# A spectral filter and a gated unit: four-channel words in the relayout, tables by TensorE, set-up inside the plan

## The chip, the cores and the metric

The kernel runs on one core of one Trainium2 chip. The metric is device microseconds of one execution, as the median of several. A core has TensorE (PE, with its weight loads as PEld), VectorE (DVE), ScalarE (ACT), GpSimd (POOL) and SyncE (SP). Here SP issues stores and on-chip relays by DMA, and POOL issues the loads that change type.

## What is computed

The reference filters along the sequence in the frequency domain, then applies a gated linear unit with a causal convolution of five taps in its gate.

```python
X = np.fft.rfft(x, axis=1)                       # x: 8 x 3200 x 256
F = (filt_r + 1j * filt_i)[None, :, :]           # 1601 x 256
x = np.fft.irfft(X * F, n=3200, axis=1)
xp = np.concatenate([zeros(8, K - 1, 256), x], axis=1)   # K = 5
gate = 1 / (1 + exp(-sum_k conv_w[k] * xp[:, k:k + S, :]))
out = (gate * (x @ w_val)) @ w_out
```

## The kernel before, in words

Each of the 8 batches is 3200 x 256. The sequence index is split as 100 x 32 (L = 100, R = 32), and the transform is done in two stages on either side of the filter, all with matmuls against tables of sines.

Stage A of a batch:

- x comes in eight chunks (j) of four of the 32 residues, cast to bf16 (`load_x`, L160, issued by POOL; ten buffers).
- s1 (L369) multiplies a chunk by the table cf_t: two matmuls of 512 columns. Their moving operand is x seen as words of two neighbouring channels: for each channel pair, four residues, two channels, so it is read in contiguous runs of two bf16 values. The result is evicted by `so` (ACT L360 or DVE L362) into the tile so, laid out as channel pair, residue, channel.
- Four transposes of DVE (`turn`, L387) take a pair of bf16 channels as one fp32 word and exchange 32 residues with 32 partitions, from so into tt.
- s2 (L397) multiplies by w_t, per unit of two frequencies (seven units, u = 0 to 6, the last of one): eight matmuls of 256 columns on quarters of the array. They too read runs of two values. `xs` evicts; `zed` (L415) multiplies by the two filter tiles fr_t and fi_t into za and zb; `inva` (L428) multiplies by a_t and b_t; `ue` evicts; `wr` (L449, SP) writes to a scratch in DRAM, escr.

Stage B of a batch, eight chunks again:

- `lv` (L459, L460, SP) loads vt from escr, six buffers; ib (L469) multiplies by ci_t; `ye` (L479, ACT) evicts into y; `halo` copies the edge on POOL.
- `conv` (L496) is the gate's convolution by diagonal matrices dg_t; `gate` (L505, ACT) the sigmoid; `val` (L514) the product with w_val; `gv` (L524, DVE) their product; `outp` (L534) the product with w_out; `oe` evicts and `store` (L548, L549, SP) writes the output.

The order of the work of every engine is fixed when the program is built. A planner (`Plan`) simulates the tasks with costs written by hand, ranks (batches and chunks staggered), pools of buffers and times for data to land, and gives one order; each engine then executes its own part of it in that order. PSUM has four buffers of 1024 fp32, shared by all products.

Ahead of the planned part stands `setup`, emitted as a whole: the iotas and all DMA issues on POOL; on DVE the index arithmetic for cf_t, w_t, a_t, b_t and ci_t; sines on ACT. The tables w_t, a_t and b_t are each 128 x 1664: a sum of index terms (on DVE for w_t; for a_t and b_t on POOL, from a product gg that POOL makes, L272, and additions, L250, tiles tba and tbb), rounded off by three DVE steps (L208 twice, L214), and a sine. cf_t has its zeros set by four memsets of POOL (L225 to L228), which stand behind the filter loads in POOL's order. The filters come in by eight loads of POOL (L198, L200; 16 rows of 26 frequencies, every second row of the filter, forward and reversed) and four copies by SP (L203). The diagonals are 20 small multiplies of DVE (L345). The planner knows of all this only as one task, `setup`, with a landing time of 22 us, and POOL as free at 18 us.

Of the kernel before, what the change touches and what calls it, by code (L numbers as in the profile page):

```python
# [16 lines left out]
L = 100  # L17
# [85 lines left out]
def kernel(  # L103
# [25 lines left out]
    DP = D // 2  # L129
# [5 lines left out]
    a_t = cpool.tile([128, NS, 64], FP16, name="a_t")  # L135
    b_t = cpool.tile([128, NS, 64], FP16, name="b_t")
# [26 lines left out]
    gstack = ExitStack()  # L163
    g1 = gstack.enter_context(tc.tile_pool(name="gen", bufs=1, side="right"))
# [7 lines left out]
    def col(name):  # L172
        return g1.tile([128, 1], FP32, name=name)

    def setup():
        pcol = iota([128, 1], [[0, 1]], 0, "pcol", 1)
        k1f = iota([128, 2, 2, 32], [[26, 2], [0, 2], [1, 32]], 0, "k1f")
        phf = iota([128, 2, 2, 32], [[0, 2], [25, 2], [0, 32]], 25, "phf")
        for j in range(4):
            load_x(0, j)  # L180
        ki = iota([128, NS], [[1, NS]], 0, "ki")
        k2w = g1.tile([128, 2, 32], FP32, name="k2w")
        iota(None, [[0, 2], [1, 16]], 0, None, dst=k2w[:, :, 0:16])
        iota(None, [[0, 2], [-1, 16]], 31, None, dst=k2w[:, :, 16:32])
        cw2 = iota([128, 2, 32], [[1, 2], [0, 32]], 0, "cw2")
        rr = iota([128, 2, 32], [[0, 2], [1, 32]], 0, "rr")
        for j in range(4, NCH):
            load_x(0, j)
        af = iota([128, L], [[1, L]], 0, "af")
        hm = iota([128, NS], [[2, NS]], 0, "hm")  # L190

        def fsrc(f, row, ap):
            return bass.AP(tensor=f.tensor, offset=f.offset + row * D, ap=ap + [[1, D]])

        for f, dst in ((filt_r, fr_t), (filt_i, fi_t)):
            fv = dst[...].rearrange("p h m d -> p (h m) d")
            for t in range(2):
                nc.gpsimd.dma_start(out=fv[64 * t:64 * t + 16],  # L198
                                    in_=fsrc(f, t, [[100 * D, 16], [2 * D, NS]]))
                nc.gpsimd.dma_start(out=fv[64 * t + 16:64 * t + 32],  # L200
                                    in_=fsrc(f, 100 - t, [[100 * D, 16], [-2 * D, NS]]))
            for t in range(2):
                nc.sync.dma_start(out=fv[64 * t + 32:64 * t + 64], in_=fv[64 * t:64 * t + 32])  # L203

        V = nc.vector

        def ts(o, i, s, op):
            V.tensor_scalar(o, i, s, None, op0=op)  # L208

        def frac(t, n, shape):  # L210
            y = g1.tile(shape, FP32, name=f"fy{n}")
            ts(y[...], t[...], MAGIC, ALU.add)
            ts(y[...], y[...], MAGIC, ALU.subtract)
            V.tensor_tensor(y[...], t[...], y[...], op=ALU.subtract)  # L214
            return y

        idx = g1.tile([128, 2, 2, 32], FP32, name="idx")
        V.scalar_tensor_tensor(idx[...], k1f[...], pcol[:, 0:1], phf[...], op0=ALU.mult,
                               op1=ALU.add)
        ts(idx[...], idx[...], 0.01, ALU.mult)  # L220
        f = frac(idx, "f", [128, 2, 2, 32])
        nc.scalar.activation(cf_t[...].rearrange("p h c i -> p (h c i)"),
                             f[...].rearrange("p h c i -> p (h c i)"), AF.Sin,
                             scale=6.2831850)
        nc.gpsimd.memset(cf_t[:, :, :, NS:32], 0.0)  # L225
        nc.gpsimd.memset(cf_t[:, 0, 1, 0:1], 0.0)
        nc.gpsimd.memset(cf_t[:, 1, 1, 24:25], 0.0)
        nc.gpsimd.memset(cf_t[:, 1, :, 25:26], 0.0)  # L228

        ge = []  # L230
        for i, v in enumerate((31.5, 63.5, 95.5)):
            t = col(f"ge{i}")
            ts(t[...], pcol[...], v, ALU.is_ge)
            ge.append(t)
        hi = ge[1]
        cc, lo, q16 = col("cc"), col("lo"), col("q16")
        V.tensor_tensor(cc[...], ge[0][...], ge[1][...], op=ALU.subtract)
        V.tensor_tensor(cc[...], cc[...], ge[2][...], op=ALU.add)
        ts(lo[...], cc[...], -32.0, ALU.mult)
        V.tensor_tensor(lo[...], lo[...], pcol[...], op=ALU.add)  # L240
        V.scalar_tensor_tensor(lo[...], hi[...], -64.0, lo[...], op0=ALU.mult, op1=ALU.add)
        ts(q16[...], lo[...], 15.5, ALU.is_ge)
        k2p = col("k2p")
        V.tensor_scalar(k2p[...], lo[...], -2.0, 47.0, op0=ALU.mult, op1=ALU.add)
        V.tensor_tensor(k2p[...], k2p[...], q16[...], op=ALU.mult)
        V.tensor_tensor(k2p[...], k2p[...], lo[...], op=ALU.add)

        def table(dst, e1, e2, name, adder):
            t = g1.tile([128, NS, 64], FP32, name="tb" + name)
            adder.tensor_tensor(t[...], e1, e2.unsqueeze(1).to_broadcast((128, NS, 64)),  # L250
                                op=ALU.add)
            y = frac(t, "t", [128, NS, 64])
            nc.scalar.activation(dst[...].rearrange("p s k -> p (s k)"),
                                 y[...].rearrange("p s k -> p (s k)"), AF.Sin,
                                 scale=6.2831850)

        e1 = g1.tile([128, NS], FP32, name="e1")
        h26 = col("h26")
        ts(h26[...], hi[...], 26.0, ALU.mult)
        V.tensor_scalar(e1[...], ki[...], h26[:, 0:1], lo[:, 0:1], op0=ALU.add, op1=ALU.mult)  # L260
        ts(e1[...], e1[...], 1.0 / N, ALU.mult)
        e2 = g1.tile([128, 2, 32], FP32, name="e2")
        wph = col("wph")
        V.tensor_scalar(wph[...], cc[...], -0.25, 0.25, op0=ALU.mult, op1=ALU.add)
        V.tensor_scalar(e2[...], k2w[...], lo[:, 0:1], 1.0 / R, op0=ALU.mult, op1=ALU.mult)
        V.scalar_tensor_tensor(e2[...], cw2[...], 0.25, e2[...], op0=ALU.mult, op1=ALU.add)
        ts(e2[...], e2[...], wph[:, 0:1], ALU.add)
        table(w_t, e1[...].unsqueeze(2).to_broadcast((128, NS, 64)),
              e2[...].rearrange("p c k -> p (c k)"), "w", V)

        gg = g1.tile([128, NS, 64], FP32, name="gg")
        nc.gpsimd.tensor_tensor(  # L272
            gg[...], hm[...].unsqueeze(2).to_broadcast((128, NS, 64)),
            rr[...].rearrange("p c k -> p (c k)").unsqueeze(1).to_broadcast((128, NS, 64)),
            op=ALU.mult)
        ts(gg[...], gg[...], 1.0 / N, ALU.mult)
        kp, aph = col("kp"), col("aph")
        V.scalar_tensor_tensor(kp[...], k2p[...], 100.0, hi[...], op0=ALU.mult, op1=ALU.add)
        ts(kp[...], kp[...], 1.0 / N, ALU.mult)
        V.tensor_scalar(aph[...], cc[...], 0.25, 0.25, op0=ALU.mult, op1=ALU.add)  # L280
        ea = g1.tile([128, 2, 32], FP32, name="ea")
        eb = g1.tile([128, 2, 32], FP32, name="eb")
        V.tensor_scalar(ea[...], rr[...], kp[:, 0:1], aph[:, 0:1], op0=ALU.mult, op1=ALU.add)
        V.scalar_tensor_tensor(ea[...], cw2[...], -0.25, ea[...], op0=ALU.mult, op1=ALU.add)
        bph = col("bph")
        V.tensor_scalar(bph[...], q16[...], 0.5, 0.25, op0=ALU.mult, op1=ALU.add)
        ts(eb[...], ea[...], bph[:, 0:1], ALU.add)
        table(a_t, gg[...], ea[...].rearrange("p c k -> p (c k)"), "a", nc.gpsimd)
        table(b_t, gg[...], eb[...].rearrange("p c k -> p (c k)"), "b", nc.gpsimd)

        vg = iota([128, 1], [[0, 1]], 0, "vg", 1)
        vi, vh, vc = col("vi"), col("vh"), col("vc")
        ii = g1.tile([128, 1], I32, name="ii")
        ts(ii[...], vg[...], 1.0, ALU.mult)
        ij = g1.tile([128, 1], I32, name="ij")

        def bits(o, shift, mask):
            src = ii
            if shift:
                ts(ij[...], ii[...], shift, ALU.logical_shift_right)  # L300
                src = ij
            if mask:
                ts(ij[...], src[...], mask, ALU.bitwise_and)
            V.tensor_copy(o[...], ij[...])
        bits(vi, 2, 0)
        bits(vh, 1, 1)
        bits(vc, 0, 1)
        kv, ph, wt, mt = col("kv"), col("ph"), col("wt"), col("mt")
        V.scalar_tensor_tensor(kv[...], vh[...], 26.0, vi[...], op0=ALU.mult, op1=ALU.add)
        V.tensor_scalar(ph[...], vc[...], 25.0, 25.0, op0=ALU.mult, op1=ALU.add)  # L310
        V.tensor_scalar(wt[...], kv[...], 50.5, 2.0, op0=ALU.is_lt, op1=ALU.mult)
# [356 lines left out]
```

## Time and profile before

| what | us |
|---|---|
| runs | 378.3, 375.16, 382.08 |
| median | 378.3 |
| profiled execution, own time | 377.58 |
| its span | 375.8 |
| PE busy | 308.6 |
| DVE busy | 279.3 |
| ACT busy | 267.5 |
| POOL busy | 71.3 |
| mean granted clock of TensorE | 0.928 |

The span runs from the first to the last instruction of the profiled execution; its own time has a little around it. In a row of the timeline the first number is the start from the span's beginning and the second the time that the group took; instructions overlap in their engine's pipeline, so the distance between two starts is what one costs in a row of them. [...] The granted clock is a share of full speed.

### The profile page before, as it was taken

Reading aid. Unit: us, or ns where it says so; the run is one execution under the profiler, and the core shown is the slowest. Engines: PE = TensorE matmul, PEld = TensorE weight load, DVE = VectorE, ACT = ScalarE, POOL = GpSimd, SP = SyncE. Lnnn points to the kernel's source line nnn. Section 1 sums busy time; section 2 is a strip of 40 time slices with the busy share of each in tenths; the row PEclk is TensorE's granted clock in tenths of the full one; section 3 lists DMA queues with packets and bytes.
Section 4 is the critical chain, followed back from the end, with each engine's and each line's share of the span. In section 5 each row is a group of like instructions: output and inputs, shape, how many; then the busy total and the mean of one; then the engine's idle time right before and its main releaser. Section 6 shows DMA issues by size and latency. Waiting matters only on the chain.

```text
span 375.8 us, 9658 instructions
## 1 busy us (share of the span) xinstructions
PE 308.6 (82%) x3936; PEld 190.5 (51%) x3936; DVE 279.3 (74%) x365; ACT 267.5 (71%) x302; POOL 71.3 (19%) x128
## 2 busy tenths in 40 slices
PE   0340158496999999899999999899999999999993
PEld 0000013124656675466656665567566767777662
DVE  8299987889457898487878797779697989834531
ACT  1231138586879797678878997789788978887673
POOL 9696612030112110210021101200010001001000
PEclk9985558877899999899999999999999999999998
DMA  7999979479679986989779986985485548868644
GB/s 111 148 127 154 153 134 165 137 113 261 186 186 233 258 212 154 221 245 211 195 145 260 246 220 144 262 250 164 143 255 153 165 144 269 238 178 242 202 129 136
DMA packets 57997, 70.91 MB, mean 189 GB/s; under 512 B 8160, under 2 KB 38368, under 8 KB 57824
## 3 DMA queue, kind: packets, MB, share of 16 engines
q1 hardware_dynamic: 44896, 55.20, 49.7%
q0 software_dynamic: 13056, 15.08, 31.2%
q8 instruction: 31, 0.51, 0.6%
q14 instruction: 14, 0.11, 0.1%
HBM read 43.78 MB, written 39.85 MB: 223 GB/s over the span
## 4 chain that ended last, share of the span: by engine, by line
PE 55%; DVE 21%; DMA 9%; ACT 5%; issue 4%; POOL 3%; SPq 1%; POOLq 0%; ACTq 0%; DVEq 0%
PE ps L534 13%; PE ps L496 11%; PE ps L369 9%; PE ps L514 7%; DMA vt<-escr 7%; DVE tt L387 7%; PE ps L397 6%; PE ps L469 5%; PE ps L428 4%; DVE gv L524 4%; DVE dg_t L345 3%; DMA xt<-in_x_dram 2%; ACT so L360 2%; DVE so L362 1%; ACT o L360 1%
## 5 line engine op out<-in xcount | busy, mean ns | idle before, releaser
L369 PE MATMUL ps<-xt,cf_t 100*128 100x512 bf16 x128 | 64.5, 609 | 36.2 <-DVE so L362 18.7
L524 DVE TENSOR_TENSOR gv<-ps,gt 128x800 bf16<-128x800 f32 x64 | 62.7, 981 | 23.1 <-PE ps L514 14.8
L360 ACT ACTIVATE so<-ps 128x1024 bf16<-128x1024 f32 x50 | 51.1, 1024 | 40.1 <-PE ps L369 25.8
L362 DVE CAST xs<-ps 128x1024 bf16<-128x1024 f32 (+1 forms) x44 | 50.5, 1147 | 35.2 <-PE ps L397 34.7
L360 ACT ACTIVATE o<-ps 100x1024 f32<-100x1024 f32 x59 | 60.7, 1028 | 18.5 <-PE ps L534 14.2
L534 PE MATMUL ps<-wo_t,gv 128*100 128x256 bf16 x512 | 69.0, 278 | 1.5 <-DVE gv L524 1.0
L160 POOL DMA_DIRECT2D xt<-in_x_dram x64 | 36.9, 579 | 158.1 <-PE ps L369 156.2
L496 PE MATMUL ps<-yt,dg_t 64*64 64x400 bf16 x1280 | 66.6, 337 | 0.0
L534 PEld LDWEIGHTS <-gv 128*100 128x100 bf16 x512 | 54.3, 126 | 21.6 <-issue 12.7
L505 ACT ACTIVATE gt<-ps 128x800 bf16<-128x800 f32 x64 | 53.6, 839 | 4.6 <-PE ps L496 3.7
L479 ACT ACTIVATE yt<-ps 128x800 bf16<-128x800 f32 x64 | 53.2, 837 | 4.7 <-PE ps L469 4.6
L514 PE MATMUL ps<-yt,wv_t 128*128 128x400 bf16 x256 | 53.9, 333 | 0.0
L360 ACT ACTIVATE u<-ps 128x1024 bf16<-128x1024 f32 (+1 forms) x46 | 44.6, 975 | 6.0 <-PE ps L428 3.2
L469 PEld LDWEIGHTS <-vt 104*128 104x128 bf16 x512 | 31.1, 102 | 30.9 <-issue 22.2
L397 PE MATMUL ps<-tt,w_t 64*64 64x256 bf16 x416 | 36.0, 412 | 12.9 <-DVE tt L387 10.1
L496 PEld LDWEIGHTS <-dg_t 64*64 64x64 bf16 x1280 | 33.7, 107 | 16.4 <-issue 2.8
L387 DVE STREAM_TRANSPOSE tt<-so 128x1024 f32<-128x1024 f32 x32 | 38.7, 1227 | 2.7 <-ACT so L360 2.6
L369 PEld LDWEIGHTS <-cf_t 100*128 100x128 f16 x128 | 12.0, 104 | 56.0 <-DMA xt<-in_x_dram 19.6
L469 PE MATMUL ps<-ci_t,vt 104*128 104x100 f16 x512 | 34.5, 213 | 5.5 <-DMA vt<-escr 5.5
L415 DVE TENSOR_TENSOR za<-xs,fr_t 128x1024 bf16<-128x1024 bf16 (+1 forms) x56 | 36.1, 649 | 3.5 <-ACT xs L360 2.3
L415 DVE TENSOR_TENSOR zb<-xs,fi_t 128x1024 bf16<-128x1024 bf16 (+1 forms) x56 | 35.5, 640 | 0.0
L428 PE MATMUL ps<-zb,b_t 64*64 64x256 bf16 x416 | 28.2, 279 | 4.4 <-DVE zb L415 4.4
(106 smaller groups left out, 222.4 us busy)
## 6 DMA issues: line engine op xcount, KB each, us to landing
out_dram<-o SPq DMA_DIRECT2D x64, 384.0 KB
xt<-in_x_dram POOLq DMA_DIRECT2D x64, 200.0 KB, 6.1
escr<-u SPq DMA_DIRECT2D x48, 256.0 KB
vt<-escr SPq DMA_DIRECT2D x64, 192.0 KB
escr<-u SPq DMA_DIRECT2D x8, 128.0 KB
vt<-escr SPq DMA_DIRECT2D x64, 16.0 KB
out_dram<-o SPq DMA_DIRECT2D x64, 16.0 KB
fr_t<-in_filt_r_dram POOLq DMA_DIRECT2D x4, 208.0 KB, 11.5
```

The source lines that it names most:

```text
L360: nc.scalar.activation(dst, src, AF.Copy, **kw)
L362: nc.vector.tensor_copy(dst, src)
L369: nc.tensor.matmul(ps[:, 512 * h:512 * h + 512], lhsT=cf_t[0:L].rearrange("p h c i -> p (h c i)"), rhs=xv[:, 64 * h:64 * h + 64], start=Tr ...
L387: nc.vector.transpose(dst, src)
L397: nc.tensor.matmul(ps[64 * t:64 * t + 64, 512 * h + D * a:512 * h + D * a + D], lhsT=w_t[rows, i, :], rhs=t_[rows, :, i, :], start=True, s ...
L415: (nc.vector if e == "DVE" else nc.gpsimd).tensor_tensor(z[:, :, 0:nm * D], xs_[:, :, 0:nm * D], f[:, :, m0:m0 + nm, :].rearrange("p h m d ...
L469: nc.tensor.matmul(ps[:, o:o + L], lhsT=v[0:NV, a, 128 * dh:128 * dh + 128], rhs=ci_t[0:NV, :], start=True, stop=True)
L496: nc.tensor.matmul(ps[64 * dh:64 * dh + 64, 512 * r:512 * r + RC * L], lhsT=dg_t[rows, dh, k, :], rhs=y[rows, dh, RC * j + k:RC * j + k + ...
L505: nc.scalar.activation(g[...], ps[:, :].rearrange("p (h n) -> p h n", h=2)[:, :, 0:RC * L], AF.Sigmoid)
L514: nc.tensor.matmul(ps[:, 512 * eh:512 * eh + RC * L], lhsT=wv_t[:, dh, 128 * eh:128 * eh + 128], rhs=y[:, dh, H + RC * j:H + RC * j + RC, ...
L524: nc.vector.tensor_tensor(gv_[...], ps[:, :].rearrange("p (h n) -> p h n", h=2)[:, :, 0:RC * L], g[...], op=ALU.mult)
L534: nc.tensor.matmul(ps[0:L, D * a:D * a + D], lhsT=gv_[:, eh, L * a:L * a + L], rhs=wo_t[:, eh, :], start=(eh == 0), stop=(eh == 1))
```

## The change

Six things change together.

1. Words of four channels (E = 4) instead of two in s1's moving operand, in the layouts of so and tt, and so in s2's moving operand, which are now read in runs of four values. The transposes still take fp32 words; source and destination are seen as channel quad, word of the quad, residue, so the innermost step is two words.
2. Of the three tables only w_t is made from index terms. Frequencies are numbered by half (t) and then in order, in place of alternately. a_t and b_t come from w_t by matmuls with a small matrix j2 (identity and a signed swap), and are evicted in four pieces each, b_t with a sign per row.
3. The 20 multiplies for dg_t become two with broadcast operands. Rounding is one fused step in place of two. cf_t's zeros are set on its argument, by DVE.
4. The filters are loaded in two cuts (6 and 7 of 13 frequencies per half), by 32 loads on POOL in place of 8, half of them contiguous; eight copies by SP in place of four.
5. The set-up's steps are tasks of the planner with ranks, costs and landing times of their own; s1 depends on its x chunk and cf_t alone, products on the filter cut and the table piece that they need. The loads of w_val and w_out move behind loads of the next x.
6. vt has four buffers in place of six; the set-up's tiles stay allocated, and w_t's intermediate lies in a buffer of y.

The core of the diff:

```diff
-    a_t = cpool.tile([128, NS, 64], FP16, name="a_t")
+    a_t = cpool.tile([128, 2, NM, 64], FP16, name="a_t")
 def frac(t, n, shape):
-    ts(y[...], t[...], MAGIC, ALU.add)
-    ts(y[...], y[...], MAGIC, ALU.subtract)
+    V.tensor_scalar(y[...], t[...], MAGIC, MAGIC, op0=ALU.add, op1=ALU.subtract)
+    FCUT = [(0, 6), (6, NM)]
+    def pool_setup():
...
+        for m0, m1 in FCUT:
+            nm = m1 - m0
+            for f, dst in ((filt_r, fr_t), (filt_i, fi_t)):
+                for t in range(2):
+                    p = 64 * t
+                    k = NM * t + m0
+                    for h in range(2):
+                        nc.gpsimd.dma_start(
+                            out=dst[p:p + 16, h, m0:m1, :].rearrange("p m d -> p (m d)"),
+                            in_=fsrc(f, k + NS * h, [[100 * D, 16], [1, nm * D]]))
+                    nc.gpsimd.dma_start(
+                        out=dst[p + 16:p + 32, 0, m0:m1, :],
+                        in_=fsrc(f, 100 - k, [[100 * D, 16], [-D, nm], [1, D]]))
+                    nc.gpsimd.dma_start(
+                        out=dst[p + 16:p + 32, 1, m0:m1, :],
+                        in_=fsrc(f, 100 - k - NS, [[100 * D, 16], [-D, nm], [1, D]]))
+    def sp_setup():
...
+        for m0, m1 in FCUT:
+            for dst in (fr_t, fi_t):
+                for t in range(2):
+                    p = 64 * t
+                    nc.sync.dma_start(out=dst[p + 32:p + 64, :, m0:m1, :],
+                                      in_=dst[p:p + 32, :, m0:m1, :])
+    TCH = [(0, 4), (4, 8), (8, 12), (12, NM)]
+    def tab_pe(i):
+        m0, m1 = TCH[i]
+        ps = psum()
+        for m in range(m0, m1):
+            for h, t in ((0, 0), (1, 1), (0, 1), (1, 0)):
+                rows = slice(64 * h, 64 * h + 64)
+                o = 512 * h + 128 * (m - m0)
+                nc.tensor.matmul(ps[64 * t:64 * t + 64, o:o + 128],
+                                 lhsT=w_t[rows, NM * t + m, :],
+                                 rhs=g["j2"][rows].rearrange("p b k -> p (b k)"),
+                                 start=True, stop=True)
+    def tab_ev(i, w, e):
...
+        if w == 0:
+            copy(e, dst, src)
+        elif e == "ACT":
+            nc.scalar.activation(dst, src, AF.Copy, scale=g["sg"][:, 0:1])
+        else:
+            ts(dst, src, g["sg"][:, 0:1], ALU.mult)
+    def diag():
+        for r in range(2):
+            rows = slice(64 * r, 64 * r + 64)
+            V.tensor_tensor(
+                dg_t[rows].rearrange("p h k j -> p (h k) j"),
+                g["ident"][rows, 64 * r:64 * r + 64].unsqueeze(1)
+                .to_broadcast((64, 2 * K, 64)),
+                g["cw"][rows].rearrange("p h k -> p (h k)").unsqueeze(2)
+                .to_broadcast((64, 2 * K, 64)), op=ALU.mult)
-    NVB, NGB, NOB = 6, 3, 3
+    NVB, NGB, NOB = 4, 3, 3
 def s1(b, j):
-        xv = xt[0:L].rearrange("p r (q e) -> p q r e", e=2)
+        xv = xt[0:L].rearrange("p r (q e) -> p q r e", e=E)
 def so(b, j, e):
-            st["SO", b] = sopool.tile([128, DP, R, 2], BF16, name="so")
+            st["SO", b] = sopool.tile([128, DQ, R, E], BF16, name="so")
 def turn(b, q):
-            st["T", b] = tpool.tile([128, DP, 32, 2], BF16, name="tt")
-        w = DP // 4
-        src = st["SO", b][:, w * q:w * q + w].rearrange("p q r e -> p (q r e)").bitcast(FP32)
-        dst = st["T", b][:, w * q:w * q + w].rearrange("p q r e -> p (q r e)").bitcast(FP32)
+            st["T", b] = tpool.tile([128, DQ, 32, E], BF16, name="tt")
+        w = DQ // 4
+        src, dst = (t_[:, w * q:w * q + w].rearrange("p q r e -> p (q r e)").bitcast(FP32)
+                    .rearrange("p (q r w) -> p q w r", r=32, w=E // 2)
+                    for t_ in (st["SO", b], st["T", b]))
         nc.vector.transpose(dst, src)
 def s2(b, u):
-                i = 2 * (m0 + a) + t
+                i = NM * t + m0 + a
-            dep = [f"lx{b},{j}"] if b else ["setup"]
+            dep = [f"lx{b},{j}"] if b else [f"x0{j}", "cfa"]
+            half = 0 if m0 + nm <= FCUT[0][1] else 1
-    add("setup", {"none": 0.0}, -100, [], None, land=22.0)
-    add("pool", {"none": 0.0}, -100, [], None, land=18.0)
+    add("pool", {"none": 0.0}, -100, [], None, land=26.0)
+    add("wts", {"POOL": 8.0}, 8.5, ["pool"], lambda e: load_w())
+    for j in range(NCH):
+        add(f"x0{j}", {"none": 0.0}, -100, [], None, land=4.5 + 1.3 * j)
+    add("fl0", {"none": 0.0}, -100, [], None, land=26.0)
+    add("fl1", {"none": 0.0}, -100, [], None, land=34.0)
+    add("pc", {"none": 0.0}, -100, [], None, land=1.5)
+    add("cfd", {"DVE": 2.0}, -50, ["pc"], lambda e: cf_dve())
+    add("cfa", {"ACT": 0.35}, -50, ["cfd"], lambda e: cf_act())
+    add("wd", {"DVE": 7.5}, -49, ["cfd"], lambda e: w_dve())
+    add("wa", {"ACT": 1.65}, -49, ["wd"], lambda e: w_act())
+    add("ey", {"DVE": 0.9}, -48, ["wd"], lambda e: eye())
+    for i in range(len(TCH)):
+        add(f"tp{i}", {"PE": 1.2}, 0.5 + 4 * i, ["wa", "ey"], lambda e, i=i: tab_pe(i),
+            take=("ps",), mode=1)
...
+    add("cid", {"DVE": 3.5}, 9, ["pc"], lambda e: ci_dve())
...
+    add("dg", {"DVE": 1.6}, 10, ["pc"], lambda e: diag(), )
     order = plan.run()
+        pool_setup()
+        sp_setup()
```

Left out above: the index arithmetic of the tables (`cf_dve`, `w_dve`, `ci_dve`, `eye`), some 60 small DVE steps in place of about as many, and the dependencies of inva, ib and conv on their table pieces.

More of the change, by code (lines that the diff above doesn't have):

```diff
@@ L220, in setup @@
[L220 to L228, printed above, removed]
@@ L266, in setup @@
[L266 to L275, printed above, removed]
@@ L284, in setup @@
[L284 to L292, printed above, removed]
```

283 lines of the change are left out of this document (152 added, 131 removed).

## The prediction

> **What bounds the kernel now.** The page first: who is busy, and when.
>
> ```profile
> PE 308.6 (82%) x3936; PEld 190.5 (51%) x3936; DVE 279.3 (74%) x365; ACT 267.5 (71%) x302; POOL 71.3 (19%) x128
> ...
> PEclk9985558877899999899999999999999999999998
> ```
>
> PE leads, but its clock row is full only after slice 10 (each 9.4 us): there are two stages. For the first I read the chain of waits up to 97 us, in order of time.
>
> ```profile
> 20.45 7.93 DVE dg_t L345
> ...
> 42.22 4.63 DVE so L362 x4
> ...
> 46.87 4.63 DVE tt L387 x4
> ...
> 83.71 8.38 DMA vt<-escr
> ```
>
> Set-up holds the start. One small multiply sits on DVE for 7.93 us, exactly while POOL makes tba and tbb; half of batch 0's stage-1 evictions stand behind the whole set-up in DVE's order until 42.2; the transposes end at 51.5. The first v load leaves at 83.7, because in SP's order it follows two writes of batch 1; the first inverse product (ib, L469) starts at 92.2.
>
> For the second stage I read PE's timeline. One slot (one of 8 chunks of a batch) repeats every 4.8 us:
>
> ```profile
> 172.13 1.04 PE L369 MATMUL ps<-xt,cf_t 100*128 100x512 bf16 x2
> 173.00 0.53 PE L469 MATMUL ps<-ci_t,vt 104*128 104x100 f16 x8
> 173.46 1.04 PE L496 MATMUL ps<-yt,dg_t 64*64 64x400 bf16 x20
> 174.33 0.69 PE L397 MATMUL ps<-tt,w_t 64*64 64x256 bf16 x8
> 174.78 0.34 PE L428 MATMUL ps<-za,a_t 64*64 64x256 bf16 x4
> ...
> 176.97 1.04 PE L369 MATMUL ps<-xt,cf_t 100*128 100x512 bf16 x2
> ```
>
> ```profile
> 172.13:176.97 4.84, 4.84 (x67) 3.19 (x66) 3.42 (x6) 4.35 (x6) 0.55 (x1) 1.00 0.95 229
> ```
>
> Columns: length, busy PE, PEld, DVE, ACT, POOL, granted clock, DMA share, GB/s. PE has no gap: PE bounds this stage, with ACT at 4.35 and DMA at 0.95 x 4.84 = 4.6 close behind. In the slot s1 takes 0.87 (172.13 to 173.00) and s2 0.45.
>
> Last, why s1 is slow: 512 columns per 0.435 us, while L428 passes 4 x 256 columns on four quarters of the array each 0.11. Look at them under both clocks.
>
> ```profile
> 43.40:44.60 1.20, 1.03 (x2) 0.23 (x2) 1.20 (x3) 0.00 (x0) 0.55 (x1) 0.50 1.04 145
> 58.90:60.60 1.70, 1.70 (x33) 1.44 (x36) 1.70 (x3) 0.57 (x1) 0.61 (x2) 0.50 0.84 113
> ```
>
> ```profile
> 43.50 1.03 PE L369 MATMUL ps<-xt,cf_t 100*128 100x512 bf16 x2 [18.75 <-DVE so L362]
> ```
>
> At clock 0.50 an s1 pair takes 1.03, at 1.00 (above) 1.04. L428, whose moving operand is contiguous, goes from 0.42 a group at 58.9 to 0.28 at 79.8. So s1 is limited by its reading, not by the array: 256 runs of two channels in 0.435 us, 1.70 ns a run. s2 reads runs of two as well and shows the same half rate.
>
> **The change part by part.** A count of slots carries the sum: from 97 to 304 us 344 of L534's matmuls (8 a slot) make 43 slots in 207 us, 4.81 each, with stage A (s1, s2, inva) beside stage B; from 304 to the end 168 make 21 in 72 us, 3.43 each, nearly all B alone. 97 + 43 x 4.81 + 21 x 3.43 = 375.8, the span. The profiled execution took 377.58, so 1.8 lie around it; the median of the runs shown is 378.3, 0.2% more.
>
> *Words of four.* Runs of four channels, half as many. Bounds: no gain, if the limit is per element (0.85 ns each); the array's rate, if it is per run (128 x 1.70 = 218 ns for 512 columns, and half of 0.435 is also what L428's rate gives). I take the run, since the time is the same at both clocks: a pair goes from 0.87 to 0.44, s2 from 0.45 to 0.23. PE's slot becomes 4.84 - 0.43 - 0.22 = 4.19. Then ACT's 4.35 is next. DMA packet time averages 4.38 over seven such slots (share 0.81 to 0.97 at 4.4 to 4.84 us), the same bytes per slot. I take 4.40. Bounds 4.19 to 4.81.
>
> [...] A penalty on top of streaming is the third rival below.
>
> *Transposes* (32 x 1.23 us) now step 8 bytes over 4-byte words. No row shows that. Below: nothing gained, the same 1024 words. Nearest rows: 1.20 ns a word now, 1.13 ns in the 1664-wide additions, and no DVE row slower. I take 1.23; doubled is the upper end, 4.9 us a batch on DVE. The evictions so write runs of 16 instead of 8 with the same 1024 elements: 1.02 and 1.22 as now.
>
> *Tables.* Gone: POOL gg, tba, tbb (2.99 + 3.73 + 3.70), on DVE 1.10 and twice 3.90, on ACT twice 1.59. New: 52 matmuls of 128 columns, at half of L428's cold 0.055 us per 128 columns some 2.9 us; 8 evictions of 512 (0.60 on ACT, 0.66 on DVE), 4.5 us; six small DVE steps of 0.24. They fall between 12 and 22 us, before filters allow the first product; without that cover up to 4.5 us. The fused rounding step saves 1.0.
>
> *Diagonals.* 20 multiplies (12.3 us, 7.9 of them stuck) become 2 of 640 elements, at 1.13 ns a word 0.8 each. *ci_t* keeps some 27 steps of 0.15. DVE's set-up then ends near 18 us instead of 42. The memsets for cf_t leave POOL, where they ran at 15.6 behind eight filter loads; s1 can start when its x lands.
>
> *Filter loads.* 8 DMAs on POOL become 32: 32 x 0.60 = 19.1 us from 7.3, with the waits seen there (0.5 to 1.3 each, four times) about 28; SP's copies go from 4 to 8 at 0.5. Writes of batch 0 and batch 1's x stand behind them. Batch 1's x left at 36.6 before, so it gains; the eight weight loads (0.75 each) follow ten x loads and land by 28 + 5.5 + 6 + 7.7 = 47, before the first val. Landing: fr's copies were issued at 18.77 and 22.7, fi's at 26.6 and 35.9. The first cut has as many bytes as one table (12/13), so 23 plus 3 for its copies, 26; the second 36. Bound below: the end of issue less the stalls, 28; above: 44, if sixteen-row pieces share worse.
>
> *The new start.* x7 lands at 14.8 as before; s1 and so 2.1, 16.9; transposes 4.63, 21.6; s2 and its eviction by 24: hidden behind the filters' 26. The second cut (36) is late next: 3.5 units of two multiplies at 0.60 are 4.2, then inverse, eviction and write 1.8: 42. From last write to first v load 4.8 (264.6 to 269.4), from there to ib 6.0 (5.1 to 7.1 in later batches): 52.8, with a us of slip 54 instead of 92.2. Bounds: 46 with filters at 28; 75 with filters at 44, transposes doubled (4.9) and v loads again 7.4 late behind batch 1's writes (before, batch 0's last inverse ended at 70, its write at 71.5, 4.8 on is 76.3; the load left at 83.7).
>
> *Buffers.* v from 6 to 4: four B slots are 13.7 us, a load takes at most 7.1, so nothing; were the loads late, up to 1 us a batch. The scratch for w_t in y's buffer is free long before batch 1 needs it: nothing.
>
> *Sum.* At 54 only s1 of batches 0 and 1 is done, at 97 before also batch 2's: 51 slots with A, 13 without. 54 + 4.8 (first ib to full slots, as 92.2 to 97) + 51 x 4.40 + 13 x 3.43 = 327.8, and 1.8: 329.6.
>
> **Rivals.** (1) *Reading does not get faster*: the limit is per element. For: no row has runs of four. Against: nothing in the rows but the unchanged time at both clocks, which fits either. 58.8 + 51 x 4.81 + 44.6 + 1.8 = 350.5.
> (2) *The start stays late*, at 75: for it, the 9 us between fi's two copies, and SP's fixed order; against it, the planner now knows of the filters (26 and 34), so batch 1 comes later in its order and batch 0's v loads ahead of batch 1's writes. 79.8 + 224.4 + 44.6 + 1.8 = 350.6.
> (3) *A fixed penalty per run on top of streaming*: 213 + 222 now, so 213 + 111 = 324 ns; slot 4.84 - 0.22 - 0.11 = 4.51, 335.2. Against: at clock 0.50 it would make a pair longer by 0.4 us, and it is not. [...]
> (4) *Slower*: the transposes at an 8-byte step. With d more each, start 4d later, and DVE, 3.72 a slot in the long run (154.7 of 200 us), becomes the bound at 3.72 + 0.5d. 385.9 is reached when 294.9 + 29.5d equals it, d = 3.1, so 4.3 us each, 3.5 times today's. For: no row excludes it. Against: no DVE row is above 1.2 ns a word.
> (5) *It does not do what it says*: no faster reading and a late start, 371.5, about no change.
>
> **How the numbers follow.** Forecast 0.63, (1) 0.12, (2) 0.12, (3) 0.04, (4) 0.05, (5) 0.04. Time 329.6. The range takes the bounds of start and slot: 46 + 4.8 + 51 x 4.2 + 44.6 + 1.8 = 311 below, and (1) and (2) above: 310 to 352; the forecast's own range is 311 to 342. A difference within 2%, 371 to 386, could not be told from no change. Faster 0.91, same 0.04 (5), slower 0.05 (4).
>
> **What would show it.** An s1 pair spaced 0.44 in a full-clock slot, s2 0.23; a slot near 4.4 in which PE has gaps that end on ACT or a DMA; transposes at 1.23; dg_t two rows under 1 us; first transposes near 17, ib near 54; the wait for the second cut of fr or fi as the longest before the first inva. Wrong: pairs still at 0.87; transposes over 2 us; v loads queued on SP behind batch 1's writes; slots at 4.8 with PE idle, which would say that ACT or DMA had been the bound all along.

## The result and the profile after

| kernel | median us | runs | ratio to before, 95% interval |
|---|---|---|---|
| before | 378.28 | 375.16 to 382.08 | 1 |
| after | 347.16 | 346.47 to 348.16 | 0.9205 [0.9143, 0.9267] |

The change is faster by 31 us. The forecast was 329.6 (310 to 352): direction and range hold, and the time is 17.6 longer than the forecast. The profiled execution after took 346.47, its span is 344.8.

Lines of the changed kernel have other numbers: s1 L417, transposes L436, s2 L446, inva L477, the write to escr L498, the loads of v L508 and L509, ib L518, conv L545, val L563, gv L573, outp L583; `so`, `u` and `o` are evicted at L408 (ACT) or L410 (DVE).

The page of after, the rows that answer to those of before, and its DMA row:

```profile
PE 288.3 (84%) x3988; PEld 191.6 (56%) x3988; DVE 256.4 (74%) x340; ACT 267.8 (78%) x309; POOL 68.0 (20%) x142
...
PEclk9999999969999999899989998999999999999997
DMA  6999999995899989898869969795677568778544
```

PE works 20 us less and is as large a share of the span as before. The DMA row stands at 9 through most of the first half. A full slot on PE's timeline, from one s1 to the next:

```profile
148.61 0.61 PE L417 MATMUL ps<-xt,cf_t 100*128 100x512 bf16 x2
149.06 0.52 PE L518 MATMUL ps<-ci_t,vt 104*128 104x100 f16 x8
149.51 1.04 PE L545 MATMUL ps<-yt,dg_t 64*64 64x400 bf16 x20
150.38 0.39 PE L446 MATMUL ps<-tt,w_t 64*64 64x256 bf16 x8
150.60 0.28 PE L477 MATMUL ps<-za,a_t 64*64 64x256 bf16 x4
...
152.72 0.61 PE L417 MATMUL ps<-xt,cf_t 100*128 100x512 bf16 x2
```

s1 takes 0.45 from start to start (148.61 to 149.06) where it took 0.87, s2 0.22 (150.38 to 150.60) where it took 0.45, and the slot 4.11. Not all slots are like this. The stretches (length, busy PE, PEld, DVE, ACT, POOL, granted clock, DMA share, GB/s; the share is the packets' time by that of the DMA engines, and it comes to more than 1 in some stretches, 1.08 from 40 to 60 us):

```profile
70.00:80.00 10.00, 5.25 (x87) 3.71 (x91) 3.49 (x5) 3.72 (x5) 0.97 (x2) 0.66 0.87 234
...
140.00:160.00 20.00, 19.83 (x316) 14.66 (x315) 18.36 (x22) 19.08 (x23) 2.21 (x4) 1.00 0.93 238
160.00:180.00 20.00, 15.07 (x196) 9.73 (x197) 12.81 (x15) 13.17 (x16) 3.51 (x8) 0.91 0.75 191
```

PE is full within a batch and idle 4.9 of 20 us where one batch follows another. What it waits for there and in the start, in the view of waits (total us, times, longest), and in the chain of waits in order of time:

```profile
PE ps L518 <- DMA vt<-escr: 16.4, 6, 7.3
PE ps L417 <- DMA xt<-in_x_dram: 11.2, 8, 6.0
```

```profile
26.16 5.19 DMA fi_t<-in_filt_i_dram
34.36 11.60 DMA xt<-in_x_dram
...
61.45 1.03 ACT u L408
...
62.50 0.36 SPq L498
...
63.07 11.63 DMA vt<-escr
```

The chain's long steps before 80 us are now transfers: a filter, an x chunk of batch 1, the first v. The write at 62.50 is the first of batch 1; in SP's order it stands ahead of the first v load and had to wait for its u. Before, the long steps were DVE's set-up; of the whole chain DMA is 24%, before 9%.

To compare kernels I cut the span in three by two starts that the view of a line gives: the first conv matmul (slots are full from there) and the last inva matmul (stage A ends). Between them lie 50 chunks in each kernel: 400 of the 512 matmuls of outp, at 8 a chunk.

| kernel | first ib | first conv | last inva | between | rest of the span |
|---|---|---|---|---|---|
| before | 92.2 | 95.7 | 330.2 | 234.5 | 45.6 |
| E = 4 alone (b_e4) | 91.1 | 95.0 | 318.1 | 223.1 | 45.8 |
| after without E = 4 (a_e2) | 74.9 | 79.3 | 314.9 | 235.6 | 45.1 |
| after | 74.8 | 79.1 | 299.7 | 220.6 | 45.1 |
| after, E = 8 (a_e8) | 71.1 | 78.0 | 319.4 | 241.4 | 45.1 |
| a_land | 70.9 | 75.5 | 302.9 | 227.4 | 45.2 |
| a_x3up | 66.0 | 70.1 | 301.7 | 231.6 | 45.1 |
| a_x3o5 | 67.2 | 71.0 | 298.7 | 227.7 | 45.2 |
| a_fbytes | 68.6 | 73.5 | 296.3 | 222.8 | 45.1 |
| a_st4 | 74.8 | 79.4 | 296.2 | 216.8 | 43.5 |

The 31.0 us of span are 16.6 of start, 13.9 in the 50 chunks (4.69 to 4.41 each) and 0.5 of rest.

### The profile page after: what moved, and what is told of

Read it like the earlier page. It is cut to its first block, busy times and chain, and to the rows that moved or that the text cites. A ratio compares the mean times of both kernels' runs of the same rounds, so it can differ in the third digit from the quotient of the medians.

```text
span 344.8 us, 9785 instructions
## 1 busy us (share of the span) xinstructions
PE 288.3 (84%) x3988; PEld 191.6 (56%) x3988; DVE 256.4 (74%) x340; ACT 267.8 (78%) x309; POOL 68.0 (20%) x142
## 2 busy tenths in 40 slices
DMA packets 57421, 70.91 MB, mean 206 GB/s; under 512 B 8608, under 2 KB 37152, under 8 KB 57376
## 4 chain that ended last, share of the span: by engine, by line
PE 43%; DMA 24%; DVE 15%; ACT 7%; issue 4%; POOL 4%; SPq 1%; ACTq 0%; POOLq 0%; DVEq 0%
DMA vt<-escr 13%; PE ps L583 12%; PE ps L545 10%; DMA xt<-in_x_dram 6%; PE ps L563 6%; DVE tt L436 5%; DVE gv L573 5%; PE ps L417 5%; PE ps L518 5%; PE ps L477 4%; DMA fi_t<-in_filt_i_dram 3%; PE ps L446 3%; ACT o L408 2%; DVE xs L410 2%; POOL xt L161 2%
## 5 line engine op out<-in xcount | busy, mean ns | idle before, releaser
L573 DVE TENSOR_TENSOR gv<-ps,gt 128x800 bf16<-128x800 f32 x64 | 62.7, 980 | 19.9 <-PE ps L563 13.6
L408 ACT ACTIVATE o<-ps 100x1024 f32<-100x1024 f32 x59 | 61.0, 1035 | 16.9 <-PE ps L583 12.9
L410 DVE CAST xs<-ps 128x1024 bf16<-128x1024 f32 (+1 forms) x44 | 50.4, 1145 | 29.0 <-PE ps L446 29.0
L583 PE MATMUL ps<-wo_t,gv 128*100 128x256 bf16 x512 | 68.7, 278 | 2.7 <-DVE gv L573 1.1
L545 PE MATMUL ps<-yt,dg_t 64*64 64x400 bf16 x1280 | 67.3, 339 | 0.3
L408 ACT ACTIVATE so<-ps 128x1024 bf16<-128x1024 f32 x53 | 54.5, 1029 | 15.9 <-PE ps L417 11.1
L583 PEld LDWEIGHTS <-gv 128*100 128x100 bf16 x512 | 54.5, 125 | 18.6 <-DVE gv L573 9.0
L161 POOL DMA_DIRECT2D xt<-in_x_dram x64 | 35.4, 556 | 124.5 <-PE ps L417 119.8
L417 PE MATMUL ps<-xt,cf_t 100*128 100x512 bf16 x128 | 47.5, 462 | 12.2 <-DMA xt<-in_x_dram 11.2
L563 PE MATMUL ps<-yt,wv_t 128*128 128x400 bf16 x256 | 54.4, 335 | 0.5 <-ACT gt L554 0.5
L408 ACT ACTIVATE u<-ps 128x1024 bf16<-128x1024 f32 (+1 forms) x46 | 44.9, 982 | 7.2 <-PE ps L477 6.6
L518 PE MATMUL ps<-ci_t,vt 104*128 104x100 f16 x512 | 34.3, 212 | 16.5 <-DMA vt<-escr 16.4
L518 PEld LDWEIGHTS <-vt 104*128 104x128 bf16 x512 | 29.6, 100 | 30.1 <-DMA vt<-escr 19.8
L545 PEld LDWEIGHTS <-dg_t 64*64 64x64 bf16 x1280 | 34.5, 108 | 17.3 <-issue 4.2
L436 DVE STREAM_TRANSPOSE tt<-so 128x1024 f32<-128x1024 f32 x32 | 40.6, 1272 | 3.2 <-ACT so L408 3.2
L477 PE MATMUL ps<-zb,b_t 64*64 64x256 bf16 x416 | 29.7, 294 | 4.4 <-DVE zb L464 4.4
L477 PE MATMUL ps<-za,a_t 64*64 64x256 bf16 x416 | 30.3, 298 | 2.4 <-DVE za L464 2.1
L446 PE MATMUL ps<-tt,w_t 64*64 64x256 bf16 x416 | 24.2, 305 | 9.0 <-DVE tt L436 4.4
```

The costliest lines, as they stand in the source:

```text
L408: nc.scalar.activation(dst, src, AF.Copy, **kw)
L410: nc.vector.tensor_copy(dst, src)
L417: nc.tensor.matmul(ps[:, 512 * h:512 * h + 512], lhsT=cf_t[0:L].rearrange("p h c i -> p (h c i)"), rhs=xv[:, DQ // 2 * h:DQ // 2 * h + DQ ...
L436: nc.vector.transpose(dst, src)
L477: nc.tensor.matmul(ps[64 * h:64 * h + 64, 512 * t + D * a:512 * t + D * a + D], lhsT=tab[rows, h, m0 + a, :], rhs=zz[w][rows, h, D * a:D * ...
L518: nc.tensor.matmul(ps[:, o:o + L], lhsT=v[0:NV, a, 128 * dh:128 * dh + 128], rhs=ci_t[0:NV, :], start=True, stop=True)
```

## The experiments

The theory after the result had two parts: the wider words do what was forecast, and the start is late for a reason that the forecast had not. For that reason there were two candidates, the order that the planner chose with wrong landing times, and the bytes on the DMA queues.

**Each half of the change alone.** a_e2 is the new kernel with words of two:

```diff
-    E = 4
+    E = 2
```

> The changed kernel with words of two channels (E = 2), all else as changed. Theory: the slot is PE's, so s1 pairs go back from 0.45 to 0.87 and s2 from 0.22 to 0.45, the slot with stage A from 4.44 to 4.81, and 45 slots make 17 us: 364 us (359 to 369), transposes back from 1272 to 1227 ns. Rival: ACT and DMA bound the slot already and the reading is hidden: 346 to 351.

Measured: 363.46 (361.70 to 365.51), ratio 0.968 [0.9616, 0.9744]. b_e4 is the old kernel with words of four and nothing else changed (layouts of s1, so, tt and the view for the transposes).

> The kernel before with words of four channels alone (s1, so, turn), set-up and tables as before. Theory: 43 slots shorten from 4.81 to 4.44, 16 us, and the start, at half rate of the array, does not change: 362 us (358 to 366); the first ib stays near 92. Rival: the gain of the change is the set-up's alone: 375 to 380.

Measured: 366.38 (364.38 to 367.19), ratio 0.9748 [0.9692, 0.9804]. That is 0.4 above its range, while a_e2 is inside its own. In both pairs of the table the wider words leave the start alone and shorten the part between: by 15.0 us in the new set-up, by 11.4 in the old. The new set-up leaves the part between alone (234.5 to 235.6 with words of two) and moves the start by 16.4. So the two halves are apart, and nearly add up: by the spans the set-up alone brings 15.8 us and the words alone 11.9 of the 31.0. Which of the set-up's parts (points 2 to 6 of the change) brings how much was not tried.

**Wider still.** a_e8 is the new kernel with `E = 8`.

> The changed kernel with words of eight channels (E = 8). If a run of four already lets the array set the time (388 ns a matmul of 512 columns), s1 and s2 stay at 388 and 305 ns and the time at 345 to 349, with transposes (16-byte steps) at 1.27 us. If a run still costs something at four, s1 falls below 380 and the time with it, by some 3 us. If the transposes pay for the step, their mean goes from 1272 to 1320 ns or more, with up to 3 us on the time.

Measured: 366.29 (365.93 to 370.67), ratio 0.979 [0.9693, 0.9887]. The groups of a_e8 (busy, mean ns of one, idle before):

```profile
L436 DVE STREAM_TRANSPOSE tt<-so 128x1024 f32<-128x1024 f32 x32 | 67.4, 2112 | 2.6 <-ACT so L408 2.6
L417 PE MATMUL ps<-xt,cf_t 100*128 100x512 bf16 x128 | 46.7, 459 | 11.1 <-DMA xt<-in_x_dram 10.5 <-DVE xs L410 0.2
```

The matmul reads no faster in runs of eight than of four (459 ns, after 462, with words of two 608). The transposes pay: 2112 ns with a step of 16 bytes, 1272 with 8, 1234 with words side by side. The time, 19 us above after, was in no outcome expected (3 us more at most). The order on every engine is that of after and the other large groups keep their means, so the transposes alone are different: four a batch at 0.84 more are 0.42 a chunk, and the 50 chunks are longer by 20.8, 0.42 each. All of it came through, though DVE is busy in only 204 of those 241.5 us.

**The order of the work.** In after the eight s1 of batch 1 stand on PE, from 35.55, ahead of batch 0's last inverse products, and wait for x to land until 46. a_land tells the planner when x of batch 1 lands.

```diff
-                    take=("xt",), land=5.0)
+                    take=("xt",), land=8.8 + 0.9 * j if b == 1 else 5.0)
```

> The changed kernel, with one number of the planner altered: batch 1's x chunks land 8.8 + 0.9 j us after their issue (as the trace shows: 35.5 to 46.0 us) in place of 5.0. Theory A, the order: batch 0's units 3 to 6 stand on PE behind all eight s1 of batch 1, and its v loads on SP behind a write of batch 1, only because the planner thinks that x is there 10 us earlier; told of it, it puts them first, the last write of batch 0 leaves near 43 and the first ib starts near 57 in place of 74.8: 331 us (327 to 337). Rival B, bandwidth: filters, x and weights fill the DMA engines until 60 us whatever the order; ib stays after 70 and the time at 345 to 349.

Measured: 348.96, with runs from 342.28 to 352.75; the profiled execution, 349.8, is 7.5 above the shortest, so its times may lie late. On SP the order became what was wanted (the first v load is issued at 56.6, before batch 1's first write), and the first ib came at 70.9, not near 54. The filter's second cut kept `zed` waiting until 42.0, u's evictions waited twice 3.5 us for writes to escr, and at the end PE's own order held it. In PE's timeline of a_land:

```profile
65.51 3.60 PE L417 MATMUL ps<-xt,cf_t 100*128 100x512 bf16 x8
...
70.94 0.51 PE L518 MATMUL ps<-ci_t,vt 104*128 104x100 f16 x8 [0.48 <-ACT u L408]
```

By the trace's landing times of its two loads the first v had landed at 65.45, 9.3 us sooner than in after (74.71), and the ib then stood behind s1 and inverse products of later batches. So the 3.8 us that the first ib came sooner are not what the order is worth: this run takes one order that held the start away and puts another in its place. What a better order would give stays open.

**The bytes of the start.** The first three runs tell little of it, since their edits did something else as well. a_nofilt leaves the filter loads out and puts two memsets in their place (its filters are not the reference's):

> The new kernel without its filter loads: two memsets of 0.5 stand in their place, so the filters' values are not the reference's; nothing else is changed. The theory, that the start is held by the bytes on the DMA queues (the queue of x and filters alone took 72 to 81% of the DMA engines from 15 to 75 us), expects x of batch 1 to land by about 35 us instead of 46, the last write of batch 0 near 47 (before: 54.0), the first L518 matmul at 58 (54 to 64; before: 74.75), and 333 us (327 to 340). The rival, that the first inverse matmul waits for work on PE, DVE and ACT of the cold start, expects it after 70 and a time of 343 or more.

It took 345.97 (343.48 to 352.55), ratio 0.9128 [0.9046, 0.921]; the profiled execution is the longest of the four. While POOL ran the two memsets (7.18 to 18.42), one DVE step of 100 elements stood still for 11.2 us, and the tables and transposes came 10.8 us later (first s2 at 34.13 for 23.33): another late start in place of the one taken away. One thing it shows: batch 0's writes had all landed by 60.3 there, and the first v load left only at 66.33, behind a write of batch 1 issued at 65.74. With the filters gone SP's order held that load, by 6 us; its product followed 4.9 us later, at 71.3. In a_x2late and a_x3late one batch's x was to wait for batch 0's halo:

```diff
-                add(f"lx{b},{j}", {"POOL": 0.6}, t0 + j - 9, ["pool"], lambda ...
+                add(f"lx{b},{j}", {"POOL": 0.6}, t0 + j - 9, ["pool"] + (["ha0"] if b == 2 else []), lambda ...
```

> The new kernel with the loads of batch 2's x made to wait for the halo of batch 0, so that none is on the queues while batch 0 is read back. If the bytes of x(2) and x(3), issued from 50 to 66 us, are what stretches the way from the first v load to its matmul to 11.6 us, it falls to about 6 and the first L518 matmul comes at 66 to 69 instead of 74.75; but the L417 matmuls of batch 2, which ran in that time, then come into the full slots: 8 of 0.9 us, which takes back most of it: 345 us (340 to 349). If the bytes are not the cause the first L518 matmul stays at 74 or later and the time grows by the 7 us of moved work, to 352 or more.

> The same with batch 3's x instead of batch 2's: the seven loads issued from 56 to 66 us go, those from 50 to 54 stay. The theory of the bytes expects 8 to 9 us from the first v load to its matmul instead of 11.6, the first L518 matmul at 71 to 73, and 344 us (341 to 347); the L417 matmuls of batch 3 did not run before the full slots anyway, so no work moves. The rival (another cause of the long landing) expects 74 to 76 and 347, no change.

They took 364.37 (363.22 to 367.32), ratio 0.9649 [0.9571, 0.9726], and 357.95 (357.53 to 358.84), 0.9471 [0.9394, 0.9548]. The planner put the next batch's loads in the free buffers, POOL's timeline shows as many x loads before the halo as in after, and a batch was overtaken by the next one: the edit did not remove what it was to remove. The first ib stayed (76.9 and 74.5).

Two clean ones followed. a_x3up holds back all batches from the third on (`if b >= 3`): every engine but POOL keeps its order, and ten x loads move behind the halo of batch 0.

> The new kernel with the loads of x of all batches from the third on (numbers 3 to 7) behind the halo of batch 0 on the POOL queue, so that batch order is kept. Only POOL's order differs from the new kernel: the ten x loads that it issues last before the halo of batch 0 (to 65.8 us) come behind it, after 76 us. The theory of the bytes expects v of batch 0 to land 3 to 5 us sooner, the first L518 matmul at 70 to 72 instead of 74.75 and 343 us (340 to 346). The rival, that the landing of the writes and loads of batch 0 does not depend on what else is on the queues, expects 74 to 76 and 347 (345 to 350).

Measured: 347.84 (344.66 to 349.79), ratio 0.9191 [0.9103, 0.9279]. From the first v load to its matmul it took 5.0 us instead of 11.7 and the first ib came at 66.0, sooner than the theory had it; the time is the same, as the rival had it. In a_x3up the SP row is the first v load, the PE rows are the first ib and a later wait, the ACT row what that wait hangs on:

```profile
61.10 0.34 SPq L508 DMA_DIRECT2D vt<-escr  x1
```

```profile
66.05 0.51 PE L518 MATMUL ps<-ci_t,vt 104*128 104x100 f16 x8 [0.45 <-ACT xs L408]
...
92.24 1.88 PE L545 MATMUL ps<-yt,dg_t 64*64 64x400 bf16 x20 [6.07 <-ACT o L408]
```

```profile
91.17 1.02 ACT L408 ACTIVATE o<-ps 100x1024 f32<-100x1024 f32 x1 [6.51 <-DMA out_dram<-o]
```

The ten loads moved from before 66 us to behind the halo, which came at 68.2, and were issued from 69.9 to 78.9; after them the first output stores landed late: ACT had no free o buffer for 6.5 us and PE stood still behind it. a_x3o5 is a_x3up with five o buffers:

```diff
-    NVB, NGB, NOB = 4, 3, 3
+    NVB, NGB, NOB = 4, 3, 5
```

> The kernel that puts x of batches 3 to 7 behind the halo of batch 0, with five buffers for the output tile o instead of three; the order on every engine is that of the run with three. There the first L518 matmul came at 66.05 instead of 74.75, and then ACT waited 6.51 us at 84.7 for a store to land (its tile o) and PE 6.07 us behind it, while the ten x loads moved there landed. If the only thing that gave the gain back is this wait for a buffer, two more buffers (two slots of 3.7 us) take it away: 341 us (338 to 344). If the bytes are what is short, whichever wait shows it, the wait goes and another comes (v of batch 1, or x), and the time stays at 345 to 349.

Measured: 347.5 (345.31 to 349.49), ratio 0.9231 [0.9141, 0.9321]. The wait for o is gone and another stands in its place, 5.85 us for the first v of batch 1, in PE's timeline of a_x3o5:

```profile
100.01 0.83 PE L518 MATMUL ps<-ci_t,vt 104*128 104x100 f16 x8 [5.85 <-DMA vt<-escr]
```

Batch 1's first ib comes at 102.5 in after, 101.0 in a_x3up and 100.0 in a_x3o5, however early batch 0's was. So taking bytes out of the way of batch 0 only hands the wait on. a_fbytes takes bytes away: each filter load and copy moves one row of its 6 or 7, and `zed` uses that row for all (not the reference's filter).

```diff
-                            out=dst[p:p + 16, h, m0:m1, :].rearrange("p m d -> p (m d)"),
-                            in_=fsrc(f, k + NS * h, [[100 * D, 16], [1, nm * D]]))
+                            out=dst[p:p + 16, h, m0, :],
+                            in_=fsrc(f, k + NS * h, [[100 * D, 16], [1, D]]))
```

> The new kernel with the same number of filter loads and copies in the same places and order, but each moves one of its 6 or 7 rows of 256 values a partition: 2 of 13 of the bytes. L464 multiplies by that row for all units of a cut, so the output is not the reference's. The theory of the bytes expects x of batch 1 to land by 38 us instead of 46, the last write of batch 0 by 49 instead of 54.0, the first L518 matmul at 62 to 68 instead of 74.75, and, with 50 slots at 4.43 us behind it as in the new kernel, 332 to 340 us. The rival, that the order of the work on the engines and the number of transfers hold the start and not their bytes, expects the first L518 matmul at 72 or later and 345 or more.

Measured: 342.83 (340.12 to 345.4), ratio 0.9051 [0.8978, 0.9124]. The first v load left at 56.72 instead of 63.07, the first ib came at 68.6, 6.1 sooner and 0.6 beyond the range of the theory, the part between grew by 2.2 us, and the time is 4 us better by the medians (6 by the ratios) where 7 to 15 were expected: the right sign, and too small. With 2 of 13 of the filters' bytes the first v still took 11.9 us to its matmul, and the x loads that after issues from 50 to 66 us were still there, from 43.5 to 59.7.

**The bytes of the slots.** a_v6 gives v the old six buffers again (`NVB, NGB, NOB = 6, 3, 3`).

> The new kernel with six buffers for v instead of four, so that loads of v may be issued two chunks earlier. PE's waits for v (16.4 us in 6 waits, 7.3 the longest) lie mostly in the start, where the loads are held by the writes and by the landing and not by a buffer: 346 us (343 to 349) by the theory of the bytes. The rival, that four buffers are what holds v in the full slots now that the slots are shorter, expects 338 or less.

Measured: 350.96 (349.49 to 352.29), ratio 0.9281 [0.9211, 0.9352]: no gain, as forecast for the four buffers, and 2 us above the range, for a reason that was not looked for. a_st4 stores one row of four of each output tile, the rest of the output stays unwritten:

```diff
-        nc.sync.dma_start(out=dst[0:96], in_=o[0:96])
-        nc.sync.dma_start(out=dst[96:L], in_=o[96:L])
+        nc.sync.dma_start(out=dst[0:96, 0], in_=o[0:96, 0])
+        nc.sync.dma_start(out=dst[96:L, 0], in_=o[96:L, 0])
```

> The new kernel with stores of one row of four of each output tile: the same number of stores in the same places, with a quarter of their bytes (6.6 MB instead of 26.2, of 70.9 in all); three quarters of the output stay unwritten. No other byte changes, and none is stored before the first output at 84 us, so the start must stay: first L518 matmul at 74 to 76. If from 79 us on bytes hold the time too (DMA share 0.94 from 100 to 140 us, v late at the head of every batch), the 9 us of PE's waits for v behind 79 us go to 2 or less, the 50 slots come to 4.15 to 4.25 us instead of 4.42 and the time to 335 us (331 to 339). If the slots are held by the engines and v is late only by the order on SP, they stay at 4.4 and the time at 344 to 348.

Measured: 336.92 (334.51 to 341.35), ratio 0.8927 [0.8883, 0.8971]. The time is in the range of the theory of the bytes, 10 us below after. Of that, 1.6 is the shorter last store (rest of the span 43.5 for 45.1; the span ends 4.8 us after the last eviction in after, 3.2 here). The number of packets is that of after (57421), with 51.25 MB for 70.91, so it is bytes that went and not packets. Its profiled execution is the longest of the six, 341.35, so its rows are upper ends: 4.34 a chunk. The waits did not go where the theory said. In a_st4:

```profile
PE ps L518 <- DMA vt<-escr: 13.8, 4, 7.3
```

7.3 of it is the start's, and 6.5 are left behind 79 us, where after has 9.0 and the theory wanted 2. So bytes are a part of what stretches the slots, and a part of the wait at each batch's head remains with a quarter of the stores' bytes. What holds that part (the order on SP, or the way write, landing, load, landing itself) stays open.

## Why the prediction was right, and where it was not

**Words of four: right.** From runs of two to runs of four the time went with the number of runs, as taken: 0.45 a pair (0.87 before) for 0.44, 0.22 (0.45 before) for 0.23 in s2. The first rival (per element, 350.5) falls, and with it the fifth. The third rival, a penalty for each run beside streaming, would have made 0.65 a pair. No run shows its 222 ns of penalty beside 213 of streaming: the pair takes 0.45, and runs of eight are no faster than runs of four (459 ns a matmul, after 462), where half as many runs would again have saved.

**Transposes, tables, diagonals: right.** 1.27 a transpose for 1.23; the two diagonal products take 1.61 together for 1.6; the 52 table products take 1.60, less than the 2.9 of the sum; s2 of batch 0 starts at 23.33 where 24 was forecast for its end. Of the fourth rival the price comes at 16 bytes and not at 8, and there not by its sum: at 0.84 more a transpose that has DVE at 3.72 + 0.42 a slot, under the 4.40 and so free, and the chunk grew by 0.42. Its sentence that no DVE row is above 1.2 ns a word overlooks gv, with 981 ns for 800.

**The slot: the size right, the reason in part.** 4.41 a chunk over 50 chunks, forecast 4.40 over 51. PE's own work is 205.89 in 220.9 us, 4.12 a chunk for the 4.19 of the sum; it is idle 15.0 us there, before 6.8 in 234.8. As forecast, PE no longer sets the slot alone, and a_st4 shows that bytes are one of the things that do. But the forecast took it from ACT at 4.35 and DMA packets at 4.38 a slot. ACT's work is 191.75 us, 3.84 a chunk; the slot shown above takes 4.11 with PE full; and 9.0 of the 15.0 idle us are waits for v, each at the first ib of a batch. That 4.40 came out is thus partly luck. By the same cut the slot before was 4.69, not 4.81, and before has 50 such chunks too, so the wider words brought 13.9 us. The sum has 21 (51 x 0.41) less the 11 that eight more slots with stage A cost it, 10 in all.

**"The new start": wrong.** It had the first ib at 54 and slots full at 58.8; they were full at 79.1. That is 20.3 too late; the slots came out 3.8 below the forecast, since they were 50 and not 51, and the rest 0.5 above: 327.8 + 20.3 - 3.8 + 0.5 = 344.8, the span. Up to the first product with a filter, at 25.6 for 26, everything kept its time. What failed are four terms, all times for data to land, the third in part SP's order as well; the last two were taken from rows near 264 us of before, where the DMA share is 0.63 and not 1:

- the second filter cut "(36)": by the trace's landing time of its last copy it landed at 40.6, in a_land at 42, and the product with it starts at 42.85;
- batch 1's x, issued at 29 to 34 as taken, landed until 45.95, up to 11.6 us later, and PE's order put it ahead of batch 0's last products: last write of batch 0 at 54.0 for 42;
- "from last write to first v load 4.8" took 9.1 (54.0 to 63.07): batch 0's write of 52.0, which the load needs, landed at 62.51, and the write of batch 1 that SP's order puts ahead of the load left at 62.50;
- "from there to ib 6.0" took 11.7.

From 20 to 80 us the DMA share was 0.97 to 1.08; before, it was 1.34 from 20 to 40 and then fell to 0.86 and 0.68. With the new order x of three batches, the filters, the weights and batch 0's writes and loads all fall into the same 50 us. This is the late start of the second rival (75, 350.6), and two of the three things that it named came true in part: the filters came at 40.6 (its bound 44), and the first v load left behind a write of batch 1. The doubled transposes did not come. Whether the landing or SP's order held that load cannot be told from after, where both end at 62.5; in a_nofilt it was the order. What is shown, with the order on every engine but POOL unchanged, is that bytes stretch the start: without the ten x loads the last step falls to 5.0 and the first ib comes 8.7 sooner (a_x3up), with less filter bytes the first v load leaves 6.4 and the first ib comes 6.1 sooner (a_fbytes). Both together were not tried; if they add, they are some 15 of the 20.3 us, and the rest, the part of the order in it too, is open.

**A step that the sum only implied: that an earlier first ib makes an earlier end, us for us.** a_x3up and a_x3o5 start 9.0 and 8.1 us sooner and end where after ends (0.9191 and 0.9231 for 0.9205): their 50 chunks are longer by 11.0 and 7.1. The DMA queues of after:

```profile
q1 hardware_dynamic: 45344, 55.20, 53.4%
q0 software_dynamic: 12032, 15.08, 29.0%
```

With the two small ones that is 83% of 344.8, 287 us of transfers on a DMA engine in the mean, for the same 70.91 MB as before; in stretches of 20 us from 20 to 160 us their share is 0.91 to 1.08, but for 0.75 from 80 to 100. A forecast of 329.6 asked for 0.87 over the whole span, with the last 45 us at 0.62. The 287 us are no fixed amount: before, the same bytes took 307 (81.6% of 375.8). And a like share moves fewer bytes in the start: 175 and 195 GB/s from 20 to 60 us, 238 to 256 from 100 to 160. I had put DMA into the slot (4.38), not into the start.

## What to carry to other kernels

When a change brings work forward into a start in which the DMA engines are already at a share of 1 (here 0.97 to 1.08 from 20 to 80 us), take landing times from stretches of that share (here 11.6 us for an x chunk and for a v load, not 5 to 7), add up the bytes that now fall into it, and look at what each engine's fixed order puts ahead of the first load and of its product. Moving loads out of the way did not help here: ten loads taken from before a first product to after it moved the wait to an output buffer, and from there to the next batch. Here a pair of matmuls with a moving operand of 2-byte values took 0.87 us in runs of two and 0.45 in runs of four, and a matmul took no less in runs of eight (459 ns, with four 462); a transpose of 4-byte words bore a step of 8 bytes (1.27 us, side by side 1.23) and not one of 16 (2.11).

## What the runs showed that was not expected

The step of the transpose: 1.23 us side by side (before), 1.27 at 8 bytes (after), 2.11 at 16 (a_e8), all for 1024 words a partition. Why the price comes between 8 and 16 bytes no run shows. The matmul of s1 has its edge elsewhere: 609 ns in runs of two (before), 462 in runs of four (after), 459 in runs of eight (a_e8).

A step of DVE that stands still while POOL works, in DVE's and POOL's timelines of a_nofilt:

```profile
7.28 11.21 DVE L352 TENSOR_SCALAR ix<-af,kv,ph 128x100 f32<-128x100 f32 x1 [2.81 <-POOL af L168]
```

```profile
7.18 5.65 POOL L215 MEMSET fr_t<- 128x6656 bf16 x1
12.77 5.65 POOL L216 MEMSET fi_t<- 128x6656 bf16 x1
```

In after the same step (L372, at 7.28) takes 0.33 us; here it ends when the second memset does (18.4). The 7.93 us of dg_t before the change are the same picture: it stood from 20.45 to 28.38, beside POOL's two additions (20.95 to 28.32). In both rows a step of DVE lasted until the second of two POOL instructions was done; what held it no run shows.

Slower matmuls in the start: in after, groups of L477 take 0.42 to 0.48 until 61 us and 0.27 to 0.31 from 61.2 to the idle wait at 67 us, while the granted clock of all stretches to 70 us is 1.00. The trace's first entry for the clock stands at 61.2 us (full speed), and the view counts what lies before it as 1.00. In the start that row says nothing of the matmuls' speed. From the timeline of after:

```profile
47.18 0.42 PE L477 MATMUL ps<-zb,b_t 64*64 64x256 bf16 x4
...
61.22 0.28 PE L477 MATMUL ps<-za,a_t 64*64 64x256 bf16 x4
...
74.75 0.85 PE L518 MATMUL ps<-ci_t,vt 104*128 104x100 f16 x8 [7.35 <-DMA vt<-escr]
75.53 0.43 PE L477 MATMUL ps<-za,a_t 64*64 64x256 bf16 x4
```

This idle wait cost more than its length: for 3.5 us after the 7.35 us without work L477 is back at 0.43 and L518 at 0.85 (0.52 at 149.06). The granted clock went from 1.00 to 0.50 at 71.4 us, 4.0 us into the wait, and back to 1.00 at 78.3, 3.5 us after its end; from 70 to 80 us it is 0.66 in the mean.
